# Attention and two gated MLPs in float32 on one core: the weight preparation of the second MLP in one line with two buffers a step

## The chip, the cores and the metric

The kernel runs on one core of one Trainium2 chip. The metric is the device time of one execution in microseconds (us); of several executions the median counts. Each execution with a profile also has its own time.

## The reference

Queries, keys and values are float32; the weights are 8-byte floating-point numbers, which the kernel itself turns into float32. The reference, cut to what matters:

```python
def reference(q, k, v, mem_k, mem_v, w_gate, w_val, w_out, w2_in, w2_out):
    # 4 batches, 8 heads, 768 positions of 64; chunks of 32 with 16 left, 8 right, 8 memory keys
    for c in range(24):
        scores = q[c] @ concat(mem_k, k[left:right]).T / 8
        out[c] = softmax(scores) @ concat(mem_v, v[left:right])
    x = out.reshape(3072, 512)                       # 3072 tokens
    x = (sigmoid(x @ w_gate) * (x @ w_val)) @ w_out  # d_ff 1536
    h = x @ w2_in                                    # d_ff 2048
    return (h * sigmoid(1.702 * h)) @ w2_out
```

## The kernel before

Every matrix is carried as a high and a low part in a reduced float32 format, and a product is three matrix multiplications (high times high, high times low, low times high), so that the result keeps float32 accuracy. A matmul instruction is 128 x 128 weights against 512 columns.

**The stages, in order of time.** First attention of the first tokens and the weights of the first MLP are prepared. Then the first MLP runs over blocks of 512 tokens (`first_product` lines 816 and 823, `gemm2` line 1015), and between its products stand the bursts of attention for the tokens to come (score matmuls line 550, value matmuls line 699, on the PSUM pair `both`). Up to here, at about 486 us, four of six blocks are done in this way. Blocks four and five of the first MLP, and then the whole second MLP, go by seven products in place of eight on 2 x 2 block matrices: `part_product` (line 1312) for x times the first weights, `b_product` (line 1642) for the second ones. The seven products are named m1 to m7 in the code; each needs sums and differences of blocks of weights and of x.

**Weight preparation.** `convert` turns 128 x 512 eight-byte words into float32: a load (line 289, 512 KB), `rebias` on ScalarE (line 293), `rest` on VectorE (line 298), the sign on ScalarE (line 303) or VectorE (line 307), and `join` on VectorE (line 313). `produce2` does this for two column blocks of `w2_in` and forms the seven weight blocks of a step; `prep_out` does it for two row blocks of `w2_out`, eight pairs in all: two conversions, four sums or differences (line 1394), four cuts into high and low part (lines 1408 and 1411), and four stores to `wo_dram` (lines 1418 and 1421) on GpSimd's queue. Of the eight pairs four (`NPREP`) are prepared early, during the last attention bursts, in memory that held weights of the first MLP (`home_a`: one raw buffer `p_raw`, one float buffer pair `p_f`, one buffer of differences `p_t`, one stage for the cuts). These homes become the ring `sb_r`, out of which `part_product` takes its weights. The other four come in steps 1, 4, 7 and 10 of the first twelve steps with `part_product`, with one raw buffer (`raw2`) and one stage (`home_b`). `produce2` for steps 1 and 2 of the second MLP stands in steps 2 and 5.

**What sets the order.** Nothing is issued in the order of the code. `Schedule.add` (line 43) collects tasks with an engine, an estimated duration, what they read and write, and `nbytes` for a transfer. `Schedule.run` (line 73) walks due times back from the products and then places the tasks one by one: on each engine the ready task with the earliest due time. Two fields move a task: `slack` makes it due earlier, and `hold` lets it count as ready only that many us after its inputs are there in the plan. The result is one fixed order per engine; on the chip every engine then runs its list from top to bottom, and an instruction whose input is late holds all behind it.

Of the kernel before, what the change touches and what calls it, by code (L numbers as in the profile page):

```python
# [135 lines left out]
def c_act(n):  # L136
    return 0.13 + n / 1200.0
# [7 lines left out]
def kernel(  # L145
# [115 lines left out]
    def convert(slot, src, gate=None, put=None, only=None, home=None, sign_act=False):  # L261
# [886 lines left out]
    def open_ys():  # L1148
        a, b = x_again(x0, F32, "yy")
        for i in range(6):  # L1150
            ys[i] = (a, b)[i // 4][:, i % 4]
        work["scr"] = b[:, 2:4]

# [16 lines left out]

    def split_x(m, k, st, kst, pool):
        def hi():
            nc.scalar.activation(xt[m, k][:, 0, :], st(), AF.Copy)

        def lo():
            eng = nc.gpsimd if pool else nc.vector
            eng.tensor_tensor(out=xt[m, k][:, 1, :], in0=st(), in1=xt[m, k][:, 0, :].bitcast(F32), op=ALU.subtract)

        add("act", c_act(BLK), hi, r=[kst], w=[("X", m, k)])
        add("pool" if pool else "dve", c_pool(BLK) if pool else c_dve(BLK), lo, r=[kst], w=[("X", m, k)])  # L1180

    def x_prep(b, mark=None, src=y_dram, b0=0, rk=lambda m, bb: [("y", m, bb)], slack=0.0):
        for k in range(2):
# [15 lines left out]
            def cut(m, i, pool):  # L1199
                split_x(m, k, lambda: ys[i], KYS[i], pool)  # L1200

# [23 lines left out]
    def produce(j, weights, spare=None):  # L1225
# [11 lines left out]
        def cut(ms, src, ks):  # L1237
            n = len(ms)
            if spare:
                keys = ["scr"]  # L1240

                def part(i, dtype=F32R):
                    return work["scr"].bitcast(dtype)[:, :n, i * H2 : (i + 1) * H2]
            else:
# [15 lines left out]
            def store():  # L1260
                d = j * NMP + PLACE.index(ms[0])
                all_ = work["scr"][:, :n, :] if spare else w()[:, o : o + n, :].bitcast(F32)
# [109 lines left out]

    hbs, tmps = {}, {}
    NG1 = F1
    NPREP = 4
    x1 = 1 - x0
# [8 lines left out]
    def prep_out(j, home):  # L1385
        stg, kstg = home["stage"]
        t, (k0, k1) = home["t"]
        pair = [convert(None, rows(w2_out, 2 * j + i), put=True, only=home["only"], home=home.get(i), sign_act=True) for i in range(2)]
        (wa, ka), (wb, kb) = [(x if callable(x) else (lambda x=x: x), k_) for x, k_ in pair]
# [8 lines left out]
        def cut(ms, src0, ks):  # L1398
            n = len(ms)

            def part(i):
# [20 lines left out]

            add("act", c_act(n * H2), hi, r=ks, w=kstg)
            add("dve", c_dve(n * H2), lo, r=ks, w=kstg)
# [12 lines left out]
    def prep_homes():  # L1437
        s0, s1, s2, s3 = ids[:4]
        kw = lambda x: [("w", x, 0), ("w", x, 1)]
        box = {}  # L1440

        def open_homes():
            box["raw"] = again(f"w{s0}", "p_raw", [P, 512], I64, s0 not in slot_pool)
            box["f"] = slot_again(s1, "p_f", F32)
            box["t"] = slot_again(s3, "p_t", F32)

        add("none", 0.0, open_homes, w=kw(s0) + kw(s1) + kw(s3))
        first = dict(only=None, stage=(lambda: slots[s2], kw(s2)), t=(lambda: box["t"][:, 0], kw(s3)))
        for i in range(2):
            first[i] = (lambda: box["raw"], kw(s0), lambda i=i: box["f"][:, i], ("w", s1, i))  # L1450
        then = dict(only=2, stage=(lambda: slots[E2], kw(E2)), t=(lambda: sigs[0], (("sig", 0), ("sig", 2))))
        return first, then

    home_a, home_b = prep_homes()
    for j in range(NPREP):
# [80 lines left out]
    for g in range(NG1):  # L1536
# [119 lines left out]
    def finish(c, sb, end):  # L1656
# [5 lines left out]
        for s_ in range(2):  # L1662
# [224 lines left out]
```

## Time and profile before

| | |
|---|---|
| median of 3 runs | 1142.57 us (1140.83 to 1145.26) |
| the profiled execution's own time | 1143.89 us |
| its span in the profile | 1141.8 us, mean granted TensorE clock 0.996 |
| TensorE (PE) busy | 1123.5 us, 98% |
| VectorE (DVE) busy | 846.8 us, 74% |
| ScalarE (ACT) busy | 587.7 us, 51% |
| GpSimd (POOL) busy | 154.2 us, 14% |

Busy time is the union of an engine's instructions. PEclk is the share of full TensorE speed that was granted. A row of the timeline has start, duration, engine, line, operation, output and inputs, shapes and count; in brackets stands how long the engine sat idle before it and what ended that. A trailing q in an engine's name (SPq, ACTq) is the queue that issues transfers.

### The profile page before, as it was taken

The numbers are of one execution on the slowest core, as the hardware profiler recorded it, in microseconds if no ns is written. First come the engines' busy times: TensorE is split into PE (matmuls) and PEld (weight loads), VectorE is DVE, ScalarE is ACT, GpSimd is POOL, SyncE is SP. The second block draws the span as 40 slices with busy tenths as digits, with TensorE's granted clock in tenths as the row PEclk, the third lists the DMA queues.
The fourth block names the chain that finished last, engine by engine and source line by source line (L and its number), as shares of the span: only waits on it lengthen the run. The fifth ranks groups of instructions, "written<-read, shape, count | busy, mean of one in ns | idle before, by whom it ended". The sixth has DMA issues, their size and how long they took to land.

```text
span 1141.8 us, 19490 instructions
## 1 busy us (share of the span) xinstructions
PE 1123.5 (98%) x7190; PEld 936.5 (82%) x7190; DVE 846.8 (74%) x1443; ACT 587.7 (51%) x969; POOL 154.2 (14%) x203
## 2 busy tenths in 40 slices
PE   8999999999999999989999999999999999999998
PEld 7888899988888778768888888878888888888886
DVE  7998757776677688788887877869966359675366
ACT  6887622222222444466665768657445365354452
POOL 5332343122432112100000000000000000000000
PEclk9999999999999999999999999999999999999999
DMA  9666244335433565643445857897796677876626
GB/s 213 219 205 198 73 128 103 54 65 130 103 88 80 125 172 170 205 156 121 138 154 181 293 199 257 275 328 261 223 281 205 203 202 219 237 215 196 182 76 183
DMA packets 245903, 203.13 MB, mean 178 GB/s; under 512 B 170928, under 2 KB 191920, under 8 KB 245808
## 3 DMA queue, kind: packets, MB, share of 16 engines
q1 hardware_dynamic: 202424, 165.44, 50.2%
q10 hardware_dynamic: 37368, 15.47, 5.0%
q0 software_dynamic: 6016, 20.98, 4.7%
q8 instruction: 57, 0.93, 0.3%
q14 instruction: 38, 0.31, 0.1%
HBM read 151.49 MB, written 50.33 MB: 177 GB/s over the span
## 4 chain that ended last, share of the span: by engine, by line
PE 86%; DMA 3%; issue 3%; DVE 3%; SPq 2%; ACT 1%; POOL 0%; ACTq 0%; DVEq 0%; POOLq 0%
PE bank L1312 29%; PE bank L1642 19%; PE bank L1015 14%; PE bank L816 13%; PE bank L823 6%; SPq L345 2%; PE both L699 1%; PE both L550 1%; DVE pt L665 1%; DMA p_raw<-in_moe_w_out_dram 1%; DMA raw<-in_moe_w_in_dram 1%; DMA raw<-in_k_dram 1%; PE bank L699 0%; DMA qn<-in_q_dram 0%; PE bank L880 0%
## 5 line engine op out<-in xcount | busy, mean ns | idle before, releaser
L1312 PE MATMUL bank<-sb_x,sb_r 128*128 128x512 f32 x1512 | 351.2, 391 | 6.3 <-ACT sb_s L1324 2.1
L1312 PEld LDWEIGHTS bank<-sb_x,sb_r 128*128 128x128 f32 x1512 | 284.5, 189 | 68.6 <-ACT sb_s L1324 3.0
L1642 PE MATMUL bank<-wq,w 128*128 128x512 f32 x756 | 177.7, 389 | 0.0
L1642 PEld LDWEIGHTS bank<-wq,w 128*128 128x128 f32 x756 | 142.0, 188 | 29.4
L816 PE MATMUL bank<-xh,w 128*128 128x512 f32 (+1 forms) x464 | 160.8, 358 | 2.4 <-ACT sig L840 1.9
L816 PE MATMUL bank<-xl,w 128*128 128x512 f32 (+1 forms) x464 | 159.7, 355 | 0.0
L1328 DVE TENSOR_TENSOR sb_s<-bank,sb_s 128x512 f32<-128x512 f32 x108 | 74.3, 689 | 80.1 <-PE bank L1312 70.8
L823 PE MATMUL bank<-xh,w 128*128 128x512 f32 (+1 forms) x464 | 108.3, 357 | 0.0
L816 PEld LDWEIGHTS bank<-xh,w 128*128 128x128 f32 x464 | 88.4, 190 | 15.9 <-ACT sig L840 2.3
L1015 PE MATMUL bank<-gh,wq 128*128 128x512 f32 (+1 forms) x448 | 98.6, 360 | 0.0
L816 PEld LDWEIGHTS bank<-xl,w 128*128 128x128 f32 x464 | 88.5, 191 | 12.2 <-DVE xl L756 0.2
L1324 ACT ACTIVATE sb_s<-bank 128x512 f32<-128x512 f32 x108 | 64.4, 598 | 46.8 <-PE bank L1312 45.7
L823 PEld LDWEIGHTS bank<-xh,w 128*128 128x128 f32 x464 | 78.1, 189 | 12.4
L1015 PEld LDWEIGHTS bank<-gh,wq 128*128 128x128 f32 x448 | 76.6, 189 | 12.9
L665 DVE STREAM_TRANSPOSE pt<-raw 32x256 f32<-32x256 f32 x184 | 79.6, 433 | 3.7 <-POOL raw L618 1.1
L1613 DVE TENSOR_TENSOR wq<-xh_g,wq 128x1024 fp32r<-128x1024 f32 (+1 forms) x60 | 60.4, 1007 | 24.1 <-ACT wq L1610 23.8
L1610 ACT ACTIVATE wq<-xh_g 128x1024 fp32r<-128x1024 f32 (+1 forms) x60 | 53.3, 888 | 28.4 <-PE bank L1642 27.4
L848 ACT ACTIVATE gh<-sig 128x512 fp32r<-128x512 f32 (+1 forms) x58 | 32.3, 558 | 61.0 <-DVE sig L843 53.2
L840 ACT ACTIVATE sig<-bank 128x512 f32<-128x512 f32 (+1 forms) x58 | 30.5, 526 | 63.9 <-PE bank L823 55.9
L1642 PE MATMUL bank<-wq,w_e 128*128 128x512 f32 x252 | 62.6, 390 | 0.0
L618 POOL TENSOR_TENSOR raw<-e,sm 96x448 f32<-96x448 f32 (+2 forms) x69 | 37.0, 546 | 167.5 <-DVE sm L610 132.1
L1642 PEld LDWEIGHTS bank<-wq,w_e 128*128 128x128 f32 x252 | 47.3, 188 | 10.1 <-DMA w_e<-wo_dram 0.4
(201 smaller groups left out, 1643.9 us busy)
## 6 DMA issues: line engine op xcount, KB each, us to landing
sb_r<-wc_dram SPq DMA_DIRECT2D x133, 256.0 KB
w<-wo_dram SPq DMA_DIRECT2D x63, 512.0 KB
wo_dram<-w POOLq DMA_DIRECT2D x24, 512.0 KB, 3.5
w_e<-wo_dram SPq DMA_DIRECT2D x21, 512.0 KB
raw<-in_moe_w_out_dram SPq DMA_DIRECT2D x16, 512.0 KB
raw<-in_moe_w_in_dram SPq DMA_DIRECT2D x16, 512.0 KB
wc_dram<-sb_r SPq DMA_DIRECT2D x15, 512.0 KB
wf_dram<-f POOLq DMA_DIRECT2D x24, 256.0 KB, 3.2
```

Source lines behind the costliest of these rows:

```text
L618: eng.tensor_tensor(out=dst, in0=e3()[r, :, c], in1=T["sm"][r].to_broadcast([n, H, keys[1] - keys[0]]), op=ALU.mult)
L665: nc.vector.transpose(T["pt"][r * CH : (r + 1) * CH, :, c * CH : (c + 1) * CH], T["pn"][c * CH : (c + 1) * CH, :, kb * CH : (kb + 1) * CH],)
L816: nc.tensor.matmul(bank[bk][:, :n], w[:, 0, ts[t]], x[xb][:, t, c0 : c0 + n], start=t == 0 and x is xhs, stop=False)
L823: nc.tensor.matmul(bank[bk][:, :n], w[:, 1, ts[t]], xhs[xb][:, t, c0 : c0 + n], start=False, stop=t == NK - 1)
L848: nc.scalar.activation(gh[:, :n], sig[:, :n], AF.Copy, scale=0.5)
L1015: nc.tensor.matmul(bank[into[m]][:, c0 : c0 + n], w[:, wi, m * P : (m + 1) * P], g[:, :n], start=f == 0 and j == 0 and c0 == 0, stop=f == ...
L1312: nc.tensor.matmul(bank[bk], w[:, o : o + P], xt[x, k][:, xl, :], start=first and k == 0 and wl == 0 and xl == 0, stop=k == 1 and wl == 1, ...
L1324: add("act", c_act(BLK), lambda: nc.scalar.activation(work[n], bank[bk], AF.Copy), r=[("bank", bk)], w=[n])
L1328: nc.vector.tensor_tensor(out=work[n], in0=bank[bk], in1=work[n], op=ALU.add)
L1610: nc.scalar.activation(quad[b_][:, c, 0, :], src(js), AF.Copy)
L1613: nc.vector.tensor_tensor(out=quad[b_][:, c, 1, :], in0=src(js), in1=quad[b_][:, c, 0, :].bitcast(F32), op=ALU.subtract)
L1642: nc.tensor.matmul(bank[bk], lhs, quad[b_][:, x, gl_, :], start=begin, stop=last and x == js[-1] and wl == 1, skip_group_check=not first,)
```

## The change

The planner's rules stay; the tasks change.

```diff
+CALM = 3.0
...
         if home is None:
             bits, ft, kf = lambda: (raw + xraw + sraw)[i], lambda: fts[g], ("f", g)
             kr, kr2 = ("raw", i), ("raw", i, 2)
+            if only == "ys":
+                bits, kr, kr2, i = lambda: work["ys45"].rearrange("p x c -> p (x c)").bitcast(I64), "ys4", "ys5", 0
...
-            nc.sync.dma_start(out=dst, in_=src)
+            (nc.gpsimd if home else nc.sync).dma_start(out=dst, in_=src)
...
-        add("sp", 0.45, load, r=["late"] if i > NRAW + 1 else [], w=[kr, kr2], nbytes=P * 512 * 8)
-        add("act", c_act(512), rebias, r=[kr], w=[kf])
-        add("dve", 0.42 if u < NW else 0.55, rest, r=[kr], w=[kr2])
+        calm = CALM if home else 1.5 if only in (2, "ys") else 1.0 if u >= NW else 0.0
+        q_ = ("pool", 1.0) if home else ("sp", 0.45)
+        add(*q_, load, r=["late"] if i > NRAW + 1 else [], w=[kr, kr2], nbytes=P * 512 * 8, slack=calm)
+        add("act", c_act(512), rebias, r=[kr], w=[kf], hold=calm)
+        add("dve", 0.42 if u < NW else 0.55, rest, r=[kr], w=[kr2], hold=calm)
...
-        add("act", c_act(BLK), hi, r=[kst], w=[("X", m, k)])
+        add("act", c_act(BLK), hi, r=[kst], w=[("X", m, k)], hold=hold)
...
-                split_x(m, k, lambda: ys[i], KYS[i], pool)
+                split_x(m, k, lambda: ys[i], KYS[i], pool, (2.0 if 0 < b < NB - 2 else 1.0) if i < 4 else 0.0)
...
             if spare:
-                keys = ["scr"]
+                stg, keys = stages[nstage[0] % 2]
+                nstage[0] += 1
...
-            add("act", c_act(n * H2), hi, r=ks, w=keys)
+            add("act", c_act(n * H2), hi, r=ks, w=keys, hold=1.0 if spare else 0.0)
...
-        pair = [convert(None, cols(w2_in, 2 * j + i), put=True, only=2 if spare else 1 + i) for i in range(2)]
+        pair = [convert(None, cols(w2_in, 2 * j + i), put=True, only=PAIR[i] if spare else 1 + i, sign_act=spare) for i in range(2)]
...
+    stages, nstage = [], [0]
+    PAIR = (2, "ys")
-    NPREP = 4
+    NPREP = 3
...
-            add("act", c_act(n * H2), hi, r=ks, w=kstg)
+            add("act", c_act(n * H2), hi, r=ks, w=kstg, hold=1.0)
...
-        s0, s1, s2, s3 = ids[:4]
+        s0, s1, s2, s3, s4, s5 = ids[:6]
...
-            box["raw"] = again(f"w{s0}", "p_raw", [P, 512], I64, s0 not in slot_pool)
+            for i, x in enumerate((s0, s4)):
+                box["raw", i] = again(f"w{x}", f"p_raw{i}", [P, 512], I64, x not in slot_pool)
...
-        first = dict(only=None, stage=(lambda: slots[s2], kw(s2)), t=(lambda: box["t"][:, 0], kw(s3)))
+        first = dict(only=None, stage=[(lambda: slots[s2], kw(s2)), (lambda: slots[s5], kw(s5))], t=(lambda: box["t"][:, 0], kw(s3)))
...
+    stages += [(lambda: slots[E2], [("w", E2, 0), ("w", E2, 1)]), (lambda: work["scr"].bitcast(F32R), ["scr"])]
...
-        if g % 3 == 2 and EARLY + g // 3 < PRE:
-            produce2(EARLY + g // 3, True)
-        if g % 3 == 1 and NPREP + g // 3 < NPR:
-            prep_out(NPREP + g // 3, home_b)
+        if 0 < g and EARLY + g - 1 < PRE:
+            produce2(EARLY + g - 1, True)
+        if 3 <= g < 3 + NPR - NPREP:
+            prep_out(NPREP + g - 3, home_b)
...
-            add("dve", c_dve(BLK), turn, r=[("c", c, s_)], w=keys)
+            add("dve", c_dve(BLK), turn, r=[("c", c, s_)], w=keys, hold=0.0 if end else CALM)
```

In words: three pairs of `w2_out` are prepared early instead of four, with two raw buffers and two stages, and their six loads are issued by GpSimd instead of SyncE (SP). In the steps with `part_product` the remaining work comes in one line, `produce2` in steps 1 and 2 and the five other pairs in steps 3 to 7, again with two raw buffers (`raw2` and a part of `xl_y`) and two stages (`w_e` and the rest of `xl_y`). Loads get slack and the work behind them gets hold. In `produce2` for early steps all signs go to ScalarE.

**The early loads of `w2_out`.** Before, on SP, where `p_raw` is the one raw buffer, `f` and `raw0`/`raw1` take queries and keys for attention, and `xh0_y` is x for the first `part_product`:

```order
L289 DMA p_raw_4494<-in_moe2_w_out_dram 128x512
L345 DMA f0_81<-in_q_dram 32x4x32 x3
L289 DMA p_raw_4494<-in_moe2_w_out_dram 128x512
L345 DMA f1_82<-in_q_dram 32x4x32 x12
L289 DMA p_raw_4494<-in_moe2_w_out_dram 128x512
L1189 DMA xh0_y_4337<-x_dram_66 128x512 x2
L289 DMA p_raw_4494<-in_moe2_w_out_dram 128x512 x2
L1298 DMA raw0_78<-wf_dram_67 128x512 x2
L1298 DMA raw1_79<-wf_dram_67 128x512 x2
L289 DMA raw2_80<-in_moe2_w_in_dram 128x4x128
L1189 DMA xh0_y_4337<-x_dram_66 128x512 x6
```

The changed kernel has the loads on POOL. `wo_dram` are the stores of finished cuts, from the two stages `w1` and `w14`; `raw2` is here the output of the softmax's normalisation of one attention tile (three instructions):

```order
L1432 DMA wo_dram_179<-w1_104 128x2x512
L623 TENSOR_TENSOR raw2_80<-e_97,sm_99 96x8x56
L623 TENSOR_TENSOR raw2_80<-e_97,sm_99 64x8x8
L623 TENSOR_TENSOR raw2_80<-e_97,sm_99 32x8x8
L1429 DMA wo_dram_179<-w1_104 128x512
L1432 DMA wo_dram_179<-w14_108 128x2x512
L292 DMA p_raw1_4690<-in_moe2_w_out_dram 128x512
L292 DMA p_raw0_4689<-in_moe2_w_out_dram 128x512
L623 TENSOR_TENSOR raw2_80<-e_97,sm_99 96x8x56
L623 TENSOR_TENSOR raw2_80<-e_97,sm_99 64x8x8
L623 TENSOR_TENSOR raw2_80<-e_97,sm_99 32x8x8
L1432 DMA wo_dram_179<-w14_108 128x2x512
```

SP's list between the keys and x has no `p_raw` any more; on POOL the two loads of the third pair stand ahead of the normalisation of the last tile.

**The start of `part_product` on PE.** `bank2`, `bank3` and so on are PSUM banks, `sb_x` the parts of x, `sb_r0` to `sb_r6` the ring. Before:

```order
L1015 MATMUL bank7_73<-gl0_88,w34_1634 128x512
L1312 MATMUL bank2_5408<-sb_x00_4775,sb_r0_5445 128x512 x3
L1312 MATMUL bank2_5408<-sb_x01_4873,sb_r0_5445 128x512 x3
L1312 MATMUL bank1_69<-sb_x00_4775,sb_r4_4602 128x512 x3
L1312 MATMUL bank1_69<-sb_x01_4873,sb_r4_4602 128x512 x3
L1015 MATMUL bank4_70<-gh1_87,w35_1635 128x512
```

and, twelve instructions of `gemm2` (line 1015) later, `sb_r1` and the rest of step 0. In the changed kernel:

```order
L1020 MATMUL bank7_73<-gl0_88,w34_1634 128x512
L1318 MATMUL bank2_5331<-sb_x00_4826,sb_r0_5409 128x512 x3
L1318 MATMUL bank2_5331<-sb_x01_4871,sb_r0_5409 128x512 x3
L1318 MATMUL bank3_5332<-sb_x10_4922,sb_r1_5509 128x512 x3
L1318 MATMUL bank3_5332<-sb_x11_4982,sb_r1_5509 128x512 x3
L1318 MATMUL bank2_5331<-sb_x30_5105,sb_r1_5509 128x512 x3
L1318 MATMUL bank2_5331<-sb_x31_5179,sb_r1_5509 128x512 x3
L1318 MATMUL bank0_68<-sb_x20_4997,sb_r0_5409 128x512 x3
L1318 MATMUL bank0_68<-sb_x21_5085,sb_r0_5409 128x512 x3
L1318 MATMUL bank3_5332<-sb_x40_5210,sb_r2_5536 128x512 x3
L1318 MATMUL bank3_5332<-sb_x41_5272,sb_r2_5536 128x512 x3
L1318 MATMUL bank2_5331<-sb_x50_5291,sb_r2_5536 128x512 x3
```

All of step 0 up to its sixth product stands ahead of those twelve `gemm2` instructions; a row is three matmuls.

**The loads of `w2_in` in the second MLP.** SP's list, `w23`, `w24`, `w25` and `w_e0` being fetches of prepared output weights and `sb_r` the stores of finished steps. Before:

```order
L1598 DMA w24_106<-wo_dram_179 128x1024
L1263 DMA wc_dram_178<-sb_r1_5569 128x2x512
L1598 DMA w25_109<-wo_dram_179 128x1024
L1263 DMA wc_dram_178<-sb_r3_5606 128x512
L1598 DMA w23_1428<-wo_dram_179 128x1024
L1263 DMA wc_dram_178<-sb_r2_5634 128x2x512
L289 DMA raw1_79<-in_moe2_w_in_dram 128x4x128
L1598 DMA w_e0_6871<-wo_dram_179 128x1024
L1598 DMA w24_106<-wo_dram_179 128x1024
L289 DMA raw2_80<-in_moe2_w_in_dram 128x4x128
L1263 DMA wc_dram_178<-sb_r4_4602 128x2x512
L1598 DMA w25_109<-wo_dram_179 128x1024
```

and now:

```order
L1611 DMA w24_106<-wo_dram_179 128x1024
L292 DMA raw1_79<-in_moe2_w_in_dram 128x4x128
L1611 DMA w25_109<-wo_dram_179 128x1024
L292 DMA raw2_80<-in_moe2_w_in_dram 128x4x128
L1269 DMA wc_dram_178<-sb_r4_5372 128x2x512
L1611 DMA w23_1428<-wo_dram_179 128x1024
L1269 DMA wc_dram_178<-sb_r3_5567 128x512
L1611 DMA w_e0_6866<-wo_dram_179 128x1024
L1269 DMA wc_dram_178<-sb_r5_5602 128x2x512
L1611 DMA w24_106<-wo_dram_179 128x1024
L1611 DMA w25_109<-wo_dram_179 128x1024
```

Both pieces begin with the same fetch, the eleventh. The load into `raw1` stood behind the thirteenth and stands now behind the eleventh; the load into `raw2` stood behind the fifteenth and stands now behind the twelfth.

## Rows read from the trace of the kernel before

**Rows 1.** Stretches of the span: length, busy time by engine, PEclk, DMA share, GB/s.

```profile
379.00:400.00 21.00, 19.14 (x134) 14.95 (x132) 13.10 (x27) 9.86 (x16) 1.92 (x3) 0.92 0.61 155
400.00:475.00 75.00, 74.13 (x632) 59.62 (x632) 63.53 (x131) 34.65 (x57) 16.62 (x27) 1.00 0.57 168
475.00:505.00 30.00, 25.78 (x107) 19.39 (x106) 26.61 (x50) 19.69 (x37) 2.72 (x4) 0.99 0.63 221
505.00:530.00 25.00, 25.00 (x106) 20.53 (x105) 21.19 (x42) 16.74 (x29) 0.00 (x0) 0.94 0.31 101
530.00:745.00 215.00, 214.96 (x948) 177.44 (x947) 173.73 (x303) 143.95 (x235) 10.89 (x16) 1.00 0.64 211
745.00:760.00 15.00, 12.93 (x57) 10.43 (x56) 8.46 (x18) 6.36 (x11) 0.00 (x0) 1.00 1.03 373
760.00:1135.00 375.00, 375.00 (x1656) 310.73 (x1655) 253.00 (x319) 188.25 (x273) 1.09 (x2) 1.00 0.69 210
```

**Rows 2.** Timeline of ACT and PE at the first stop, 382 to 392 us.

```profile
382.81 0.69 ACT L293 ACTIVATE p_f<-p_raw 128x512 f32<-128x512 f32 x1 [6.46 <-DMA p_raw<-in_moe_w_out_dram]
...
391.03 0.50 PE L816 MATMUL bank<-xh,w 128*128 128x512 f32 x1 [1.86 <-ACT sig L840]
```

**Rows 3.** SP's queue: its waits (us, times, longest), then its timeline.

```profile
SPq L289 <- DVE p_f L313: 32.0, 4, 16.9
SPq L1189 <- DMA x_dram<-qt: 10.5, 2, 5.4
...
448.27 21.66 SPq L289 DMA_DIRECT2D p_raw<-in_moe_w_out_dram  x2
```

**Rows 4.** Groups of instructions of the early pairs, 379 to 505 us: busy, mean ns, idle.

```profile
L303 ACT ACTIVATE p_raw<-p_raw 128x512 f16<-128x512 f32 x8 | 10.9, 1362 | 4.2 <-DVE p_raw L298 4.2
L293 ACT ACTIVATE p_f<-p_raw 128x512 f32<-128x512 f32 x8 | 5.5, 685 | 11.5 <-DMA p_raw<-in_moe_w_out_dram 10.3 <-DVE w L1411 1.2
L1408 ACT ACTIVATE w<-p_t 128x512 fp32r<-128x512 f32 x8 | 5.3, 664 | 4.7 <-DMA wo_dram<-w 3.2 <-DMA f<-in_q_dram 1.0 <-ACT f L1035 0.4
...
L313 DVE SCALAR_TENSOR_TENSOR p_f<-p_f,p_raw 128x512 int32<-128x512 int32 x8 | 5.7, 715 | 0.8 <-ACT p_raw L303 0.7
L1411 DVE TENSOR_TENSOR w<-p_t,w 128x512 fp32r<-128x512 f32 x8 | 5.5, 683 | 0.8 <-ACT w L1408 0.7
```

**Rows 5.** Timeline around the change of phase: PE, ACT, DVE, POOL.

```profile
463.44 2.07 POOL L618 TENSOR_TENSOR raw<-e,sm 96x448 f32<-96x448 f32 x3 [3.37 <-DVE sm L610]
...
470.81 0.88 PE L699 MATMUL both<-pt,vn 128*64 128x96 f32 x16
...
473.35 0.69 ACT L293 ACTIVATE p_f<-p_raw 128x512 f32<-128x512 f32 x1
...
482.20 0.69 DVE L1195 TENSOR_TENSOR xl_y<-xh_y 128x512 f32<-128x512 f32 x1 [1.05 <-DMA xh_y<-x_dram]
...
495.86 0.69 DVE L1411 TENSOR_TENSOR w<-p_t,w 128x512 fp32r<-128x512 f32 x1
...
502.03 0.63 ACT L1255 ACTIVATE sb_r<-sb_t 128x512 fp32r<-128x512 f32 x1 [1.59 <-DMA wo_dram<-w]
502.71 1.46 PE L1312 MATMUL bank<-sb_x,sb_r 128*128 128x512 f32 x4 [1.98 <-ACT sb_r L1255]
```

**Rows 6.** DMA issues, the stores of finished cuts: KB each, median us to landing.

```profile
wo_dram<-w POOLq DMA_DIRECT2D x24, 512.0 KB, 3.5
```

**Rows 7.** Timeline before the stop in the second MLP: SP, DVE, ACT, PE.

```profile
736.79 0.32 SPq L1598 DMA_DIRECT2D w<-wo_dram  x1
...
745.38 0.38 SPq L289 DMA_DIRECT2D raw<-in_moe_w_in_dram  x1
...
753.42 0.43 DVE L298 TENSOR_SCALAR raw<-raw 128x512 int32<-128x512 int32 x1 [2.04 <-DMA raw<-in_moe_w_in_dram]
753.93 1.37 ACT L303 ACTIVATE raw<-raw 128x512 f16<-128x512 f32 x1 [4.32 <-DVE raw L298]
...
757.86 2.33 PE L1312 MATMUL bank<-sb_x,sb_r 128*128 128x512 f32 x9 [2.07 <-ACT sb_s L1324]
```

More of the change, by code (lines that the diff above doesn't have):

```diff
@@ L1151, in open_ys @@
             ys[i] = (a, b)[i // 4][:, i % 4]
-        work["scr"] = b[:, 2:4]
+        work["scr"], work["ys45"] = b[:, 2:4], b[:, 0:2]
     def open_work():
@@ L1169, in open_raw, with split_x @@
         ys[4], ys[5] = fts[0], fts[1]
-    def split_x(m, k, st, kst, pool):
+    def split_x(m, k, st, kst, pool, hold):
         def hi():
@@ L1239, in cut @@
             if spare:
-                keys = ["scr"]
+                stg, keys = stages[nstage[0] % 2]
+                nstage[0] += 1
                 def part(i, dtype=F32R):
-                    return work["scr"].bitcast(dtype)[:, :n, i * H2 : (i + 1) * H2]
+                    return stg().bitcast(dtype)[:, :n, i * H2 : (i + 1) * H2]
             else:
@@ L1261, in store @@
                 d = j * NMP + PLACE.index(ms[0])
-                all_ = work["scr"][:, :n, :] if spare else w()[:, o : o + n, :].bitcast(F32)
+                all_ = stg()[:, :n, :].bitcast(F32) if spare else w()[:, o : o + n, :].bitcast(F32)
                 nc.sync.dma_start(out=wc_dram[d : d + n].rearrange("m p c -> p m c"), in_=all_)
-            add("act", c_act(n * H2), hi, r=ks, w=keys)
+            add("act", c_act(n * H2), hi, r=ks, w=keys, hold=1.0 if spare else 0.0)
             add("dve", c_dve(n * H2), lo, r=ks, w=keys)
@@ L1385, in prep_out @@
     def prep_out(j, home):
-        stg, kstg = home["stage"]
+        stgs = home["stage"]
+        nstg = nstage if stgs is stages else [0]
         t, (k0, k1) = home["t"]
-        pair = [convert(None, rows(w2_out, 2 * j + i), put=True, only=home["only"], home=home.get(i), sign_act=True) for i in range(2)]
+        pair = [convert(None, rows(w2_out, 2 * j + i), put=True, only=PAIR[i] if home["only"] else None, home=home.get(i), sign_act=True) for i in range(2)]
         (wa, ka), (wb, kb) = [(x if callable(x) else (lambda x=x: x), k_) for x, k_ in pair]
@@ L1399, in cut @@
             n = len(ms)
+            stg, kstg = stgs[nstg[0] % len(stgs)]
+            nstg[0] += 1
             def part(i):
@@ L1442, in open_homes @@
         def open_homes():
-            box["raw"] = again(f"w{s0}", "p_raw", [P, 512], I64, s0 not in slot_pool)
+            for i, x in enumerate((s0, s4)):
+                box["raw", i] = again(f"w{x}", f"p_raw{i}", [P, 512], I64, x not in slot_pool)
             box["f"] = slot_again(s1, "p_f", F32)
             box["t"] = slot_again(s3, "p_t", F32)
-        add("none", 0.0, open_homes, w=kw(s0) + kw(s1) + kw(s3))
-        first = dict(only=None, stage=(lambda: slots[s2], kw(s2)), t=(lambda: box["t"][:, 0], kw(s3)))
+        add("none", 0.0, open_homes, w=kw(s0) + kw(s1) + kw(s3) + kw(s4))
+        first = dict(only=None, stage=[(lambda: slots[s2], kw(s2)), (lambda: slots[s5], kw(s5))], t=(lambda: box["t"][:, 0], kw(s3)))
         for i in range(2):
-            first[i] = (lambda: box["raw"], kw(s0), lambda i=i: box["f"][:, i], ("w", s1, i))
-        then = dict(only=2, stage=(lambda: slots[E2], kw(E2)), t=(lambda: sigs[0], (("sig", 0), ("sig", 2))))
+            first[i] = (lambda i=i: box["raw", i], kw((s0, s4)[i]), lambda i=i: box["f"][:, i], ("w", s1, i))
+        then = dict(only="pair", stage=stages, t=(lambda: sigs[0], (("sig", 0), ("sig", 2))))
         return first, then
+    stages += [(lambda: slots[E2], [("w", E2, 0), ("w", E2, 1)]), (lambda: work["scr"].bitcast(F32R), ["scr"])]
     home_a, home_b = prep_homes()
```

## The prediction

> **What bounds the kernel now.** I read three views in this order: the busy time by stretches, then the timeline of TensorE wherever a stretch shows it idle, then back from there along the engine that it waited for.
>
> TensorE bounds it. From 530 to 745 us it is idle for 0.04 us, from 760 to 1135 us not at all [rows 1]; there its work sets the time, and the change neither adds nor removes a matmul. What can be won lies in four places. The last attention bursts: 1.86 us idle in 379 to 400 and 0.87 in 400 to 475. The change to `part_product`: 4.22 idle in 475 to 505. The second MLP: 2.07 idle in 745 to 760 [rows 1]. Twice the clock comes on top. In 379 to 400 the granted clock is 0.92 and in 505 to 530 it is 0.94, which are stretches at 1.2 in place of 2.4 GHz right behind an idle TensorE; 8% of 21 us is 1.7 us and 6% of 25 us is 1.5 us [rows 1]. In 745 to 760 an idle time of 2.07 us cost no clock [rows 1], so that price is not certain. Sum: 9.02 idle and 3.2 of clock, 12.2 us. The profiled execution took 1143.9 us, 1.3 above the median of 1142.6; with all of it gone it would take 1131.7.
>
> Why TensorE stops is the same each time: an engine with a fixed list stands at an instruction whose transfer is late, and what TensorE needs stands behind it.
> - First stop: ScalarE waits 6.46 us for `p_raw`, to 382.81, and runs late from there; TensorE waits for its sigmoid to 391.03 [rows 2].
> - Change of phase: the four early pairs go through one raw buffer. SP stands 32.0 us, 16.9 at the longest, at loads that wait for the `join` that frees it; x for `part_product` stands behind on that queue [rows 3]. The last load lands at 473.35, that pair is finished at 495.86, 22.5 us later, its store frees the ring at 502.03, and TensorE starts at 502.71 after 1.98 us [rows 5].
> - Second MLP: a load of `w2_in`, issued at 745.38, reaches VectorE at 753.42, ScalarE has stood 4.32 us at the sign behind it, and TensorE starts again at 757.86 [rows 7].
>
> **The change part by part.**
>
> *Six loads on GpSimd, two raw buffers, two stages, hold 3 us.* The issues leave SP: it no longer stands those 32.0 us [rows 3]. ScalarE's `rebias` of the first pair moves behind two more attention tiles, and its place allows the load 3 us more than the plan's estimate. That the plan was short by 6.46 us at the first stop speaks for a remainder, but this includes time that the load stood in SP's list [rows 2, 3]. Bounds for 379 to 475, which has 2.73 idle and 1.7 of clock: nothing gained or all 4.4. I take 3.5: the large stop and its clock go, and some 0.9 of small ones stay.
>
> *Three early pairs, not four.* A pair costs ScalarE at most 2 x 0.685 (rebias) + 2 x 1.362 (sign) + 4 x 0.664 (cuts, one of them narrower) = 6.8 us. VectorE has 2 x 0.715 + 4 x 0.683 = 4.2 us, and six shorter instructions (two `rest`, four differences) of at most 0.715, so 4.2 to 8.4; I take 6.4 [rows 4]. In 475 to 505 VectorE is busy 26.6 of 30 us [rows 1]; a fourth less preparation ends the backlog. The list of the changed kernel has the last value burst of attention 44 full matmuls earlier; at the 0.227 us a matmul of 948 in 215 us [rows 1] that is 10 us. In the trace it stands at 470.81, and x, which must go out to memory and come back, reaches VectorE at 482.20 [rows 5]. Ten us earlier, x is no longer what TensorE waits for. The third pair's two loads stand ahead of the last normalisation, at 463.44 before [rows 5] and some 10 earlier now, so at about 453, and land about 457 (3.5 us, [rows 6]). With the 22.5 us that the last pair took here [rows 5] it ends near 480, on the old time scale; TensorE wants the second part of the ring near 488, less the 4 us that it now comes sooner. So the margin is some 4 us, with two stages and less VectorE work on its side. Against it: the list now puts six products (36 matmuls, 8.2 us) ahead of the twelve `gemm2` matmuls that stood between, so nothing fills a gap there. Bounds for 475 to 530, which has 4.22 idle and 1.5 of clock: nothing gained or 5.7, or a loss of up to the 2.7 us of filler that moved away. I take 4.5.
>
> *Five pairs and two steps of `w2_in` in one line.* The fifth pair and three signs that move from VectorE to ScalarE (3 x 1.36 = 4.1 us) come into 530 to 745, where VectorE is busy 173.7 and ScalarE 144.0 of 215 us [rows 1]. That is room for 6.4 and 6.8 + 4.1 us. The cover is these idle shares; where a load is late they are no cover, since the engine stands. The trace shows such waits there without any idle TensorE (0.04 us, [rows 1]), so I charge one short new stop, 0.5 us; bounds 0 and 2.07, as the stop at 757 [rows 7].
>
> *Loads of `w2_in` earlier.* The load that came 4.32 us late for ScalarE moves ahead of three fetches. At 745.38 it stood behind the fifteenth fetch; the twelfth was at 736.79 [rows 7]. 8.6 us earlier is more than the 4.32 that ScalarE stood. Bounds 0 and 2.07; I take 2.0.
>
> *Holds without a transfer of their own* (cuts, x, the turn of the output): they only change places in a list. The turn stands in 760 to 1135, where TensorE is never idle and VectorE busy 253 of 375 us [rows 1]; the last block has no hold. I cost them at nothing; if that cover were gone, a store of the output would come 3 us later, off the path until the end.
>
> Sum: 3.5 + 4.5 - 0.5 + 2.0 = 9.5 us. 1143.9 - 9.5 = 1134.4 against the profiled execution, 1133.1 from the median; I say 1133.5.
>
> **A rule that speaks against it.** The stores of finished cuts, issued by GpSimd while VectorE was busy 85% of the time, landed 3.5 us after their issue [rows 1, 6]. The Trainium skill, "SBUF — State Buffer" (Summary: rules for kernel authors), says that transfers issued by GpSimd are starved while VectorE is in a fast mode, and to issue from another queue. By it the six loads come late and the first two gains shrink; by the row they do not.
>
> **The rivals.**
> - *The waits only move.* The third pair is not done when TensorE wants it, and nothing fills in. For: 36 matmuls in a row, a margin of some 4 us. Against: the two buffers. Then 475 to 530 gains nothing: 1143.9 - 3.5 - 2.0 + 0.5 = 1138.9, from the median 1137.6. Chance 0.16.
> - *Loads through GpSimd come late*, by the mechanism of the rule. ScalarE then stands as at the first stop, and 379 to 475 gains nothing and the change of phase half: 1143.9 - 2.3 - 2.0 + 0.5 = 1140.1, from the median 1138.8. For: nothing but the rule. Against: 3.5 us [rows 6]. Chance 0.06.
> - *GpSimd's list stands* and the kernel becomes slower. Place: the two loads of the third pair, ahead of the last tile's normalisation. They wait for the same `join` that held SP for up to 16.9 us [rows 3]. From normalisation to value burst there are 7.4 us (463.44 to 470.81), of which 2.07 are its own work [rows 5], and the rest is mostly transposes; so it decides from about 2 us on. Its price is up to 16.9 - 2 = 15 us of idle TensorE and one stretch at half clock, 1.7: 1143.9 - 2.0 + 15 + 1.7 = 1158.6 at worst; with half that wait, 6.5 us, 1143.9 - 2.0 + 6.5 + 1.7 = 1150.1. Against: two raw buffers, and a list that puts the loads after pair two's work. Chance 0.08.
> - *The change does not do what it says in the steps*: five pairs in a line crowd 530 to 745, and two or three stops of 2 us with a clock stretch appear: 1143.9 - 10 + 7 = 1140.9, from the median 1139.6. Chance 0.06.
>
> **How the numbers follow.** Forecast 0.64. About 0.5%, 5.7 us, is what a measurement of this kernel can tell from no change: faster is below 1136.9, slower above 1148.3. Faster: the forecast, with a little of the first rival, 0.67. Same: rest of the first, the second and fourth, 0.24. Slower: the third, 0.09. The range begins where all of the 12.2 us goes, 1142.6 - 12.2 = 1130.4, less 1 for the restarts of TensorE that idle time does not count: 1129.5. It ends at 1142.5, no change, past the first, second and fourth rival; the third is left out.
>
> **What would show it.** In the changed profile: no ScalarE wait of over 3 us for `p_raw`, and PEclk 1.00 in 379 to 475; idle TensorE under 1.5 us between 475 and 530, in place of 4.22; SP without long stands at the conversion's load line in that stretch; no stop near 757. It is wrong if TensorE is idle for several us right after its first `sb_x` matmuls, if `both` is late behind GpSimd, or if idle time appears in 530 to 745.

## The result, and the profile after

The changed kernel took 1129.08 us (median of 4 runs, 1127.70 to 1130.38), the kernel before beside it 1142.33 (4 runs): ratio 0.9881, 95% interval 0.9856 to 0.9906. It is faster by 13.3 us. The forecast was 1133.5 with a range of 1129.5 to 1142.5: the direction came out, the gain was half as large again as forecast, and the time lies 0.4 us below the range.

The profiled execution of the changed kernel took 1130.38 us, its span is 1128.6, against 1143.89 and 1141.8 before. Its busy time by the stretches of [rows 1] (length, then PE, PEld, DVE, ACT, POOL busy, PEclk, DMA share, GB/s):

```profile
379.00:400.00 21.00, 21.00 (x150) 17.14 (x149) 16.39 (x32) 6.62 (x15) 3.00 (x5) 1.00 0.71 177
400.00:475.00 75.00, 75.00 (x581) 60.75 (x580) 64.80 (x131) 38.07 (x63) 20.30 (x28) 1.00 0.52 159
475.00:505.00 30.00, 30.00 (x135) 24.82 (x134) 26.41 (x51) 22.42 (x41) 2.02 (x3) 1.00 0.56 185
505.00:530.00 25.00, 25.00 (x112) 20.71 (x111) 22.16 (x45) 15.58 (x28) 0.00 (x0) 1.00 0.30 106
530.00:745.00 215.00, 215.00 (x950) 178.03 (x949) 175.84 (x311) 148.68 (x241) 13.73 (x20) 1.00 0.70 242
745.00:760.00 15.00, 15.00 (x67) 12.40 (x67) 9.04 (x17) 12.16 (x20) 0.00 (x0) 1.00 0.43 167
```

All four places of the prediction are without idle TensorE and at a granted clock of 1.00. But count the matmuls, which from 475 us on are all 128 x 512. Without a stop one starts every 0.226 us (36 in 8.15 us, from 482.56 to 490.71, below). From 475 to 530 there were 107 + 106 before [rows 1], in one count over the 55 us 211, and now 245: 34 more, 7.7 us of work. The idle time of that stretch was 4.22 us and its clock was put at 1.5. So more came back than the prediction had on its list. The two counts, before and changed:

```profile
475.00:530.00 55.00, 50.78 (x211) 39.92 (x210) 47.81 (x91) 36.43 (x66) 2.72 (x4) 0.97 0.48 166
475.00:530.00 55.00, 55.00 (x245) 45.53 (x244) 48.56 (x95) 38.01 (x68) 2.02 (x3) 1.00 0.44 149
```

The first early pair: loads on POOL, first `rebias` on ACT.

```profile
391.37 0.58 POOL L292 DMA_DIRECT2D p_raw<-in_moe_w_out_dram  x1
395.38 0.54 POOL L292 DMA_DIRECT2D p_raw<-in_moe_w_out_dram  x1 [3.43 <-PE bank L828]
...
400.48 0.66 ACT L296 ACTIVATE p_f<-p_raw 128x512 f32<-128x512 f32 x1
```

ScalarE starts on it without a wait, where it stood 6.46 us before [rows 2]. The list of ScalarE's waits between 379 and 505 holds none for a load of `p_raw`.

The change of phase (from the first MLP to `part_product`), PE and DVE:

```profile
457.13 0.88 PE L704 MATMUL both<-pt,vn 128*64 128x96 f32 x16
468.49 0.69 DVE L1200 TENSOR_TENSOR xl_y<-xh_y 128x512 f32<-128x512 f32 x1
482.56 8.32 PE L1318 MATMUL bank<-sb_x,sb_r 128*128 128x512 f32 x36
486.48 0.69 DVE L1422 TENSOR_TENSOR w<-p_t,w 128x512 fp32r<-128x512 f32 x1
490.71 1.98 PE L1020 MATMUL bank<-gh,w 128*128 128x512 f32 x8
```

The last value burst and x's arrival at VectorE are both 13.7 us earlier than in [rows 5]. The six products run as one piece of 36 matmuls, and the last cut of the third pair, still at work at 487, holds up nothing.

The second MLP: waits between 715 and 765 us (us in total, times, longest).

```profile
DVE raw L301 <- DMA raw<-in_moe_w_in_dram: 5.7, 2, 3.8
ACT raw L306 <- DVE raw L301: 3.6, 1, 3.6
```

ScalarE still stands 3.6 us at a sign, where it stood 4.32 in [rows 7]. But this wait now ends at 734.96, 19.0 us earlier than before, while TensorE comes to the matmul of the old stop only 14.2 us earlier (743.69 for 757.86, the same matmul counted from the end). Against TensorE's work the sign comes 4.8 us sooner, and TensorE does not stop.

### The profile page after: what moved, and what is told of

It reads as the page before. It is cut to its first block, busy times and chain, and to the rows that moved or that the text cites. A ratio compares the mean times of both kernels' runs of the same rounds, so it can differ in the third digit from the quotient of the medians.

```text
span 1128.6 us, 19515 instructions
## 1 busy us (share of the span) xinstructions
PE 1116.4 (99%) x7190; PEld 933.7 (83%) x7190; DVE 842.4 (75%) x1440; ACT 589.6 (52%) x972; POOL 161.6 (14%) x209
## 4 chain that ended last, share of the span: by engine, by line
PE 97%; DMA 1%; SPq 1%; ACT 0%; DVE 0%; issue 0%; ACTq 0%
PE bank L1318 30%; PE bank L1655 20%; PE bank L1020 18%; PE bank L821 15%; PE bank L828 8%; PE both L704 2%; PE both L555 2%; SPq L350 1%; PE bank L704 1%; PE bank L885 0%; DMA kn<-in_mem_k_dram 0%; PE bank L645 0%; DMA vn<-in_v_dram 0%; DMA w<-wo_dram 0%; PE both L645 0%
## 5 line engine op out<-in xcount | busy, mean ns | idle before, releaser
L1318 PE MATMUL bank<-sb_x,sb_r 128*128 128x512 f32 x1512 | 347.4, 389 | 0.0
L623 POOL TENSOR_TENSOR raw<-e,sm 96x448 f32<-96x448 f32 (+2 forms) x69 | 41.0, 606 | 176.1 <-DVE sm L615 149.0
```

The source lines that it names most:

```text
L623: eng.tensor_tensor(out=dst, in0=e3()[r, :, c], in1=T["sm"][r].to_broadcast([n, H, keys[1] - keys[0]]), op=ALU.mult)
L1318: nc.tensor.matmul(bank[bk], w[:, o : o + P], xt[x, k][:, xl, :], start=first and k == 0 and wl == 0 and xl == 0, stop=k == 1 and wl == 1, ...
```

## The experiments

Each kernel is timed beside the kernel before on the same chip, whose medians were 1144.12 (e1 to e4), 1144.49 (e5 to e8), 1143.76 (e9 to e11) and 1144.71 us (e12, e13). So compare the ratios. The table shows where TensorE's time was lost. For 379 to 475, where matmuls of many shapes mix, I took from the trace the time from each matmul's start to the next, less the median for its line and shape, and summed it (a matmul's late start, below, is the same difference for it alone). TensorE of the changed kernel is never idle there, so its 3.6 us are no stop but the uneven spacing of attention's small matmuls, and the choice of the median moves a row by up to some 0.6 us. For the rest stands the count of matmuls in the stretch; one missing is 0.226 us lost, and one or two are the edge of the stretch.

| kernel | ratio, 95% interval | 379-475, us lost | 475-530, matmuls | 530-745 | 745-760 |
|---|---|---|---|---|---|
| before | 1 | 9.3 | 211 | 948 | 57 |
| changed | 0.9881 (0.9856-0.9906) | 3.6 | 245 | 950 | 67 |
| e1 loads on SP | 0.9903 (0.9887-0.9918) | 6.8 | 244 | 948 | 68 |
| e2 one raw buffer | 1.0008 (0.9998-1.0018) | 3.6 | 172 | 947 | 68 |
| e3 four pairs | 0.9954 (0.9942-0.9966) | 5.7 | 211 | 948 | 68 |
| e4 early part, no hold | 0.9873 (0.9858-0.9888) | 4.2 | 244 | 950 | 68 |
| e5 early part as before | 0.9894 (0.9872-0.9915) | 6.9 | 240 | 948 | 68 |
| e6 before + second raw | 1.0050 (1.0033-1.0067) | 16.4 | 236 | 941 | 64 |
| e7 later part, no hold | 0.9880 (0.9858-0.9903) | 4.8 | 243 | 940 | 68 |
| e8 later work spread | 0.9863 (0.9840-0.9887) | 4.1 | 245 | 944 | 68 |
| e9 before + three pairs | 0.9954 (0.9938-0.9970) | 6.3 | 243 | 928 | 63 |
| e10 later part alone | 0.9993 (0.9978-1.0008) | 9.2 | 197 | 949 | 68 |
| e11 two pairs | 0.9907 (0.9887-0.9927) | 3.8 | 244 | 937 | 68 |
| e12 e2 on SP | 1.0015 (1.0003-1.0027) | 3.6 | 174 | 947 | 68 |
| e13 e2, no hold | 0.9918 (0.9902-0.9934) | 3.5 | 211 | 948 | 68 |

### The early part, one feature at a time

**e1**, from the changed kernel:

```diff
-            (nc.gpsimd if home else nc.sync).dma_start(out=dst, in_=src)
+            nc.sync.dma_start(out=dst, in_=src)
...
-        q_ = ("pool", 1.0) if home else ("sp", 0.45)
+        q_ = ("sp", 0.45)
```

> The changed kernel with the six early loads of w2_out issued by SyncE again; buffers, stages, holds and the three pairs stay. My theory: SP stands again at loads that wait for the join of the pair before, with x for part_product behind them, so a stop of TensorE of 1 to 2 us comes back in 475 to 505; about 1131 us against 1129.1. Rival, by the rule that transfers issued by GpSimd are starved beside a busy VectorE: SP is the better queue, the loads land sooner, and the time is 1129 or less. Second rival: with two raw buffers the queue does not matter at all, 1129 with no stop.

1132.33 us. Its one stop of PE, and the stretch around it:

```profile
452.88 0.88 PE L704 MATMUL both<-pt,vn 128*64 128x96 f32 x16 [3.20 <-DMA vn<-in_v_dram]
```
```profile
400.00:475.00 75.00, 71.80 (x567) 58.07 (x566) 61.38 (x127) 37.22 (x60) 17.41 (x24) 1.00 0.55 166
```

The stop is larger than expected and elsewhere: at 450, at a load of `vn` that ScalarE's queue had issued at 443.15, and not in 475 to 530. Whether the loads on SP made it late no run shows. SP is not the better queue: nothing was won by leaving GpSimd, and the intervals of e1 and of the change overlap.

**e2**:

```diff
-            first[i] = (lambda i=i: box["raw", i], kw((s0, s4)[i]), ...
+            first[i] = (lambda: box["raw", 0], kw(s0), ...
```

> The changed kernel with one raw buffer for the early pairs in place of two; loads on GpSimd, two stages, holds and three pairs stay. My theory: GpSimd stands at the second load of each pair, the third pair is finished some 10 us later, and a stop of 2 to 4 us comes back at the change to part_product; 1131.5 to 1134. Rival: three pairs are so much less work that one buffer is enough, 1129 to 1130.

1145.48 us: the whole gain is gone, where I expected 2 to 4 us. One stretch of the windows, and the largest of the stops:

```profile
475.00:530.00 55.00, 44.83 (x172) 34.17 (x171) 44.33 (x87) 39.84 (x67) 3.39 (x6) 0.91 0.57 203
...
490.18 5.78 PE L1318 MATMUL bank<-sb_x,sb_r 128*128 128x512 f32 x12 [3.92 <-ACT sb_r L1261]
```

The last `p_raw` load goes out at 479.83 (443.82 in the changed kernel). 73 matmuls are missing, 16.5 us: TensorE waits for the ring, and the granted clock of 0.91, 9% of 55 us, is some 5 us of it.

**e3**:

```diff
-    NPREP = 3
+    NPREP = 4
```

> The changed kernel with four early pairs again and four later ones; the two buffers, two stages, GpSimd loads and holds stay. My theory, which gave the change of phase 4.5 us for the third pair less and its buffers together: most of it is the work that is left out, so 3 us of stops in 475 to 530 come back, about 1132. Rival: the buffers and the queue did it, and four pairs would run as well: 1129 to 1130. Second rival: the last normalisation stands behind the fourth pair's loads on GpSimd, over 1135.

1139.07 us, more than my 1132 and over the second rival's 1135, but not by that rival's way: in 475 to 530 TensorE stops once, for a `gh` of ScalarE that waits behind VectorE.

```profile
475.00:530.00 55.00, 50.36 (x211) 41.13 (x211) 49.75 (x98) 40.30 (x73) 4.03 (x6) 0.94 0.51 178
...
491.19 3.78 PE L1020 MATMUL bank<-gh,w 128*128 128x512 f32 x8 [4.64 <-ACT gh L853]
```

These are 211 matmuls, the number of the kernel before; the granted clock of 0.94 is part of the loss. With all the new buffers and queues in place, a fourth pair costs 34 matmuls, 7.7 us.

**e4**:

```diff
-        calm = CALM if home else 1.5 if only in (2, "ys") else ...
+        calm = 0.0 if home else 1.5 if only in (2, "ys") else ...
```

> The changed kernel with hold and slack 0 for the conversions of the early pairs (the holds of the cuts, of w2_in and of x stay). My theory: ScalarE's rebias stands in its list before its load has landed, waits 2 to 4 us for p_raw once or more, and a stop of 1 to 2 us in 379 to 475 comes back, with or without a stretch at half clock: 1131 to 1133. Rival: two buffers let the loads run early enough, no ScalarE wait for p_raw over 1 us, 1129.

1129.52 us, no difference, and no wait of ScalarE for `p_raw`: the rival holds. With two buffers the hold of the early conversions is worth nothing.

### Which part carries the gain

**e5**: the changed kernel with one raw buffer, one stage, loads on SP and no hold for the early pairs, but three of them.

> The changed kernel with the whole early part as it was: one raw buffer, one stage, loads on SyncE, no hold, only that three pairs are early; the later part is that of the change. My theory after the run with one raw buffer (1145.5): the buffer decides, so the loss at the change of phase comes back in full, 7 us or more of TensorE time in 475 to 530; and the stop near 389 with ScalarE waiting over 3 us for p_raw comes back too, some 4 us: 1140 to 1147 beside a kernel before of 1144. Rival: the early part gains only through the third pair less, and 1133 to 1136 remains.

1133.63 us. My theory from e2 fell: without any of the new early features 1.06% of the 1.19% are still there. Its SP and ACT waits, 379 to 510 and 379 to 475:

```profile
SPq L292 <- DVE p_f L316: 20.9, 3, 16.4
```
```profile
ACT p_f L296 <- DMA p_raw<-in_moe_w_out_dram: 10.3, 4, 3.0
```

SP stands as long at one load as in [rows 3], and ScalarE waits for `p_raw` 10.3 us, as much as in [rows 4]; the change of phase loses 5 matmuls instead of 34. At the change of phase these waits were not what TensorE paid for. In 379 to 475 it still loses 3.3 us more than the changed kernel, at two stops (0.97 and 1.87 us idle) that VectorE ends; whether the waits have a part in those is not shown.

**e6**: the kernel before with the second raw buffer in slot `s4`, nothing else.

> The kernel before with one thing changed: a second raw buffer for the early pairs (loads on SyncE, four pairs, one stage, no holds, later part as before). My theory: the buffer alone lets each load run beside the conversion before it, SP no longer stands 32 us, and half or more of the 7.6 us lost in 475 to 530 comes back: ratio to the kernel before 0.994 to 0.997. Rival: the buffer is needed but does nothing alone, because four pairs are too many for ScalarE and VectorE: ratio 0.999 to 1.002. The stop near 757 stays in both.

1150.41 us, slower by 0.5%, which neither theory had. The loss moves ahead of the change of phase (16.4 us in 379 to 475):

```profile
397.60 2.53 PE L1015 MATMUL bank<-gh,w 128*128 128x512 f32 x6 [2.59 <-ACT f L1035]
447.31 0.50 PE L816 MATMUL bank<-xh,w 128*128 128x512 f32 x1 [1.95 <-ACT sig L840]
452.54 0.50 PE L816 MATMUL bank<-xh,w 128*128 128x512 f32 x1 [2.18 <-DVE sig L843]
```

With a buffer more, the planner sets preparation earlier (the last `p_raw` load goes out at 439.70, before at 469.60), and ScalarE and VectorE then serve it ahead of the first MLP: before the stop at 447 ScalarE stood 4.40 us at a cut of an early pair, to 445.43, with the sigmoid that TensorE waits for behind it, and VectorE stood 2.92 us for the same cut.

**e9**: the kernel before with `NPREP = 3`, the five later pairs in steps 1, 3, 5, 7 and 9.

> The kernel before with three early pairs in place of four and nothing else; the five later pairs stand in steps 1, 3, 5, 7 and 9, through the one raw buffer and the one stage of before. My theory since the early part as before, with three pairs, ran at 0.9894 of the kernel before: the pair that is left out gives most of the gain by itself, 6 to 9 us: ratio 0.992 to 0.995; SP stands at p_raw loads as long as before (over 10 us at once), and 475 to 530 loses under 2 us of TensorE time. The stop near 757 stays, or another takes its place. Rival: the later part has to take the fifth pair through one buffer, and gives back what is won: ratio 0.997 to 1.002 with stops of 3 us or more in 530 to 745.

1139.06 us, ratio 0.9954: just short of the expected 0.992 to 0.995. Two of its stretches say why:

```profile
475.00:530.00 55.00, 55.00 (x243) 45.36 (x243) 49.85 (x95) 38.10 (x69) 2.02 (x3) 1.00 0.49 165
530.00:745.00 215.00, 211.99 (x928) 173.34 (x927) 172.87 (x307) 145.00 (x235) 13.72 (x20) 1.00 0.66 225
```

The change of phase is clean by this one number alone (243 matmuls). In 379 to 475 3.0 us come back too: the first `p_raw` load now goes out at 387.41 in place of 379.21, and the stop at 391 is gone. But 530 to 745 loses 20 matmuls, 4.5 us, that the kernel before did not lose. The one buffer that the fifth pair has to share is not what TensorE waits for in most of this: of its six stops up to 746 us four, with 2.89 of 3.93 us of idle time, are ended by fetches of prepared `w2_out`.

```profile
705.88 1.66 PE L1642 MATMUL bank<-wq,w 128*128 128x512 f32 x6 [0.37 <-DMA w<-wo_dram]
...
722.32 3.01 PE L1642 MATMUL bank<-wq,w_e 128*128 128x512 f32 x12 [1.19 <-DMA w_e<-wo_dram]
...
742.07 2.99 PE L1642 MATMUL bank<-wq,w 128*128 128x512 f32 x12 [0.41 <-DMA w<-wo_dram]
745.97 3.00 PE L1642 MATMUL bank<-wq,w_e 128*128 128x512 f32 x12 [0.92 <-DMA w_e<-wo_dram]
```

Why these fetches are late with a fifth pair there, no run shows.

**e10**: the changed kernel with the early part as before and four pairs.

> The changed kernel with the whole early part as before, four pairs too: what is left is the later part (line, two buffers and stages, holds) and the holds on x. My theory: the gain is that of the stop near 757 and no more, 2 us, since the loss in 379 to 530 comes back in full: ratio 0.997 to 0.999. Rival: x's holds and the later part, not the third pair less, change the lists around 475 as well, and half the gain stays: ratio 0.993 to 0.996.

1142.85 us, no difference that shows. The later part alone frees 745 to 760 (68 matmuls) and does nothing for 379 to 475; 475 to 530 becomes worse (197 against 211). e9 and e10 gain 0.46 and 0.07% apart, e5, which has both, 1.06%: the two parts need each other. Three pairs clear the change of phase and the stop at 391, and the later part lets the fifth pair in without new stops.

### The later part

**e7**:

```diff
-        calm = CALM if home else 1.5 if only in (2, "ys") else 1.0 if u >= NW else 0.0
+        calm = CALM if home else 0.0
```

> The changed kernel without slack and hold on the loads and conversions of the later part (w2_in and the five later pairs): all 0. My theory, by the prediction's fourth term: in the second MLP the loads stand behind the fetches again, ScalarE waits at a sign for its load, and a stop of about 2 us near 750 comes back, 1131 to 1132. Rival: the stop went because the later steps are emptier or the buffers are two, and nothing changes: 1129 to 1130.

1132.13 us at the same ratio as the change, 0.9880. The stop near 757 does not come back; in the trace two late starts of 1.0 and 1.1 us stand at 727 and 731 (940 matmuls in 530 to 745). Inconclusive as a time.

**e8**:

```diff
-        if 0 < g and EARLY + g - 1 < PRE:
-            produce2(EARLY + g - 1, True)
-        if 3 <= g < 3 + NPR - NPREP:
-            prep_out(NPREP + g - 3, home_b)
+        if g in (2, 5):
+            produce2(EARLY + g // 3, True)
+        if g in (1, 3, 5, 7, 9):
+            prep_out(NPREP + (1, 3, 5, 7, 9).index(g), home_b)
```

> The changed kernel with the later work spread out over the first twelve steps instead of in one line (produce2 in steps 2 and 5, the five pairs in steps 1, 3, 5, 7 and 9); buffers and holds stay. My theory: with two buffers and two stages the spacing is free, since VectorE and ScalarE have room in 530 to 745; no stop over 0.3 us there, 1129 to 1130. Rival, that the line itself is needed: loads and stages meet again and one or two stops of 0.5 to 2 us appear between 530 and 760, 1130.5 to 1132.

1130.08 us: with the buffers, stages and holds of the change the line is not needed. Its trace has one late start of 1.25 us at 733, over the 0.3 us that I expected at most; its time shows no difference.

**e11**: the changed kernel with `NPREP = 2`.

> The changed kernel with two early pairs and six later ones in steps 3 to 8. It asks how much room 530 to 745 has. My theory: the sixth pair fits too (VectorE was 82% and ScalarE 69% busy there), and no stop is left for fewer early pairs to remove: 1128.5 to 1130.5, no difference. Rival: the pairs crowd, cuts of w2_out come late for the first fetches, and a stop of 2 us or more appears in 600 to 760: 1131 or more.

1133.13 us, the rival's side of the two: one late start of 2.16 us at 676 and one of 0.70 at 718, in this stretch:

```profile
530.00:745.00 215.00, 212.46 (x937) 175.26 (x936) 175.48 (x308) 150.55 (x242) 16.78 (x24) 1.00 0.70 240
```

VectorE and ScalarE are hardly busier than with three pairs (175.84 and 148.68 us), so it is no want of room in all. At the first, TensorE waits for ScalarE, which had stood 1.88 us at a cut of a pair until 674.84; the second is a fetch of `w_e`. Two pairs are not better than three.

The holds on x and on the turn of the output, and the signs that moved to ScalarE, were taken alone in no run.

### Why one raw buffer was late in e2 and not in e5

**e12** is e2 with the loads on SP, **e13** is e2 without the slack and hold of the early loads and conversions.

> The changed kernel with one raw buffer and the early loads on SyncE; two stages, holds of 3 us and three pairs stay. One raw buffer on GpSimd with the holds cost 16 us (1145.5); one raw buffer on SyncE without holds and with one stage cost 4 (1133.6). If GpSimd's list is what stands (loads behind stores that wait for cuts, the mechanism of my slow rival), this kernel runs like the second, 1132 to 1135, with the last load before 460 us. If the hold is what delays, since with one buffer each load waits for a conversion that the plan holds back by 3 us, it runs like the first, 1142 to 1146, with the last load after 475 us.

> The changed kernel with one raw buffer on GpSimd, and no hold or slack for the early conversions; two stages and three pairs stay. The other half of the same question. If the hold is what delays, the last load comes before 463 us and the time is 1131 to 1136. If GpSimd's list is what stands, 475 to 530 loses 5 us or more again, 1138 to 1146.

1146.26 and 1135.10 us. The last `p_raw` load of e12, e13 and e5 (SPq, POOL, SPq):

```profile
480.28 0.33 SPq L292 DMA_DIRECT2D p_raw<-in_moe_w_out_dram  x1
```
```profile
470.73 0.56 POOL L292 DMA_DIRECT2D p_raw<-in_moe_w_out_dram  x1 [1.83 <-DVE p_f L316]
```
```profile
455.54 0.33 SPq L292 DMA_DIRECT2D p_raw<-in_moe_w_out_dram  x1
```

With the hold the queue changes nothing (the last load at 479.83 and 480.28). Without it the kernel is 0.9% faster, about 10 us: with one buffer every load waits for a conversion that the plan delays, and the last load of e2, whose first goes out at 389.33, is 9.1 us behind that of e13, whose first goes out at 388.98. But e13 meets only half of that expectation. Its time lies in the range, but its last load does not come before 463, and it still loses 34 matmuls at the change of phase, the sign that I had set for GpSimd's list:

```profile
475.00:530.00 55.00, 51.09 (x211) 39.81 (x210) 46.81 (x92) 40.70 (x72) 2.75 (x4) 0.97 0.46 161
```

Three things separate it from e5, where 5 are lost: the queue, the second stage and the hold of 1 us on the cuts. No run takes one alone, and it stays open. e4 and e13 differ by the raw buffer alone, both without that hold: 0.9873 against 0.9918, and 244 matmuls against 211. So beside loads on GpSimd and two stages the second buffer is worth 0.45%, about 5 us, even without the hold; beside the early part as before it is not needed (e5). The hold itself buys nothing (e4).

## Why the prediction was wrong

**What bounds the kernel: right.** TensorE, and the four places were the ones. Between 379 and 760 us every one of them was cleared.

**The size of the loss: the step that failed.** "Sum: 9.02 idle and 3.2 of clock, 12.2 us" took TensorE's idle time for what its stops cost. By the counts and start-to-start times the two profiles differ by 5.7 us in 379 to 475 (the term said 3.5, at most 4.4), 34 matmuls or 7.7 us in 475 to 530 (4.5, at most 5.7), 2 matmuls or 0.5 in 530 to 745 (a loss of 0.5) and 10 or 2.3 in 745 to 760 (2.0): 16.2 us in place of 9.5. A matmul is busy for 0.39 us and the next starts after 0.226, so idle time begins 0.16 us after the loss does. At the first stop TensorE's starts are 2.03 us late for 1.86 idle, at 757 it is 2.23 for 2.07, at the change 2.15 for 1.98; a slip under 0.16 us shows no idle time at all. I allowed 1 us for this at the bottom of the range; it was 4.0 (16.2 less 12.2). The nine stops on my list at 0.16 us each are 1.5 of these 4.0; the 0.5 in 530 to 745 was on no list; about 1 us are slips without idle time, such as 0.11 us at the matmul behind nearly every stop; the last 1 us is not placed. The rest of the error is my discount on the terms, 2.7 us below their sum: nothing was left over at the places where I held something back. Rows 1 held the better measure, 107 matmuls in 30 us. The Trainium skill, "Perfetto Trace Analysis" (Identifying the Most-Contended Engine), says that matmul busy time is no good measure of how close a kernel is to its limit, because matmuls are pipelined, and to use the share of peak reached and the busy share of weight loads. The traces agree on the latter: weight loads were busy 19.39 + 20.53 = 39.92 us in 475 to 530 [rows 1] and are now 24.82 + 20.71 = 45.53. Of the latter 12% was missing, which of 55 us is 6.8.

Of the 16.2 us 13.2 reached the span. TensorE's list is the same in both kernels for its first 3287 matmuls; that point comes at 345.08 us in the profile of before and at 346.53 in that of the change, and in the others between 343.9 and 346.0. So 1.5 us are the difference of two executions, and the profiled one was the longest of the four; of the rest some 0.6 us lie in 345 to 379 and some 1.1 behind 760.

**The change of phase: the effect right, its cause wrong.** The prediction gave it to "one raw buffer" on which SP stands 32.0 us, and to a fourth less work, without saying which. e5 and e9 keep that buffer and lose 5 and 2 matmuls, e5 with SP standing 16.4 us at once; e3 has two buffers and no `p_raw` load on SP, and loses 34; e6 adds the buffer alone and is slower. One early pair less is what decides: with four pairs no kernel gains here but e6, which loses more than that ahead of it, and with three the stretch is clean both with the early part as before (e5, e9) and with that of the change. It is no guarantee: three pairs through one buffer with the rest of the new early part lose 34 to 73 (e2, e12, e13). The third pair's loads went out 10.6 us before my estimate (442.39 against 453) and its last cut ended 7 us after it (487.2 against 480). TensorE began the six products 4.6 us before that end and did not stop, so the margin of 4 us that I worked out was not what TensorE needed.

**The first stop: half right.** It went, and with more than its size. But e9 shows it gone with loads on SP, one buffer and no hold: three pairs start 8 us later. e3 shows it gone with four pairs and the new early part: either is enough, which the prediction did not see.

**Five pairs in line: no new stop, but not for my reason.** I charged 0.5 us for a new stop, and none came. I called idle shares of VectorE and ScalarE the cover; e9 has the same shares (172.87 and 145.00 busy of 215 us) and loses 4.5 us. So the shares are no cover. The line is not what covers either (e8). What is left of the later part are its buffers and stages, its holds, without which 10 matmuls are lost (e7), and the signs on ScalarE; which of them does it is not shown.

**Earlier `w2_in` loads: right in size** (2.3 for 2.0). In part the mechanism held: against TensorE's work the sign comes 4.8 us sooner. But ScalarE still stands 3.6 us at it, and the slack and hold, which I took for the cause in e7, are not needed. The later part alone clears that stop (e10).

**The rule on GpSimd's transfers** was rightly not followed: the six loads caused ScalarE no wait, while VectorE was busy 64.80 of 75 us, and on SP they were no better (e1). They landed 4.9 us after their issue (median of six), later than the 3.5 us that I took from the stores [rows 6]; whether VectorE was in the mode that the rule speaks of, and when such loads land from SP, no run shows.

**The slow rival** did not come, and two raw buffers exclude it, as the text said. Its price was of the right order: with one raw buffer the kernel is 16.4 us slower than the change (e2). Of this some 10 us are the hold in the plan and not GpSimd's list, since the loads are as late from SP (e12); whether that list has a part in the rest stays open (e13).

## What to carry to other kernels

Size a stop of a pipelined engine by the instructions that are missing from its stretch, or by start-to-start times, not by idle time. A long wait on a queue or an engine is a cause only if what it delays is late for the bounding engine; test it by taking it away alone before building on it. Moving work off a crowded stretch pays in full only if the stretch that receives it can take it, and busy shares do not tell whether it can: here fewer early pairs alone gained 0.5%, the new later part alone nothing that shows, the two together 1.1%.

## What the runs showed of the hardware that I had not expected

For matmuls of 512 columns at the full clock, idle time understates a stop by the same amount each time: 3.20, 3.92 and 4.64 us of idle (e1, e2, e3) were late starts of 3.36, 4.08 and 4.80 us, 0.16 more each. The clock did not follow the length of a stop: after 3.20 us of idle in e1 the granted clock of 400 to 475 stayed 1.00, after 1.86 before, the stretch 379 to 400 has 0.92 [rows 1]. And the first 345 us differ by up to 2.6 us between the profiled executions (343.9 to 346.5), with the same TensorE list up to there, more than several of the differences looked for here.
